# Decode attention with a parallel MLP on one core: the output weights laid 32 rows to a partition, the attention output computed whole at the end

## The chip, the core and the metric

The kernel runs on one core of a Trainium2 chip. The metric is the time of one execution in microseconds on the device, as the median of several runs. The core has a matrix engine (TensorE, "PE" in the profile, with its weight loads as "PEld"), a vector engine (VectorE, "DVE"), a scalar engine (ScalarE, "ACT"), a general engine (GpSimd, "POOL") and a queue engine (SyncE, "SP") that here issues nearly all transfers. 16 DMA engines carry the data from HBM into the on-chip memory SBUF (128 partitions). TensorE writes its results into PSUM, which has eight banks of 512 fp32 values per partition.

## What is computed

A decode step for 4 sequences with one token each, D = 576. The normalised input xn goes through grouped-query attention (32 query heads, 16 KV heads, head size 128) over the last 2048 cached positions, and through an MLP block with a gated-shift mixer; both are added to x.

```python
def _A_ref(x, k_cache, v_cache, wq, wo):
    W = min(4096, max(256, Sk // 4))                 # 2048
    q = (x @ wq).reshape(B, Sq, Hq, Dh).transpose(0, 2, 1, 3)
    k = jnp.repeat(k_cache[:, :, Sk - W:, :], rep, axis=1)
    v = jnp.repeat(v_cache[:, :, Sk - W:, :], rep, axis=1)
    p = _softmax(jnp.einsum("bhqd,bhkd->bhqk", q, k) * (Dh ** -0.5), axis=-1)
    o = jnp.einsum("bhqk,bhkd->bhqd", p, v)
    return o.transpose(0, 2, 1, 3).reshape(B, Sq, Hq * Dh) @ wo
...
xn = _layernorm(x, axis=-1)
return x + _A_ref(xn, A_k_cache, A_v_cache, A_wq, A_wo) + _B_ref(xn, B_w1, B_w2, B_w3, B_w4)
```

`_B_ref` makes x1 = xn + (shifted gelu(layernorm(xn) @ w1)) @ w2 and returns x1 + gelu(layernorm(x1) @ w3) @ w4. With one token the shifts leave only zeros. All tensors are bf16. The K and V windows are 33.6 MB each, wo and w4 are 4096 x 576 and 4608 x 576.

## The kernel before

Every step is registered with `add(engine, function, waits, sig, key)` or `add_dma`; for each engine the steps are sorted by their key, and each waits for the named steps by semaphores. So each engine's order is fixed by hand through the keys. Two loops of four turns each run on TensorE, one over K and one over V.

Nearly all transfers are issued by SP in one order (lines 213 to 252): wq, w1, w2, w3, then the 16 K tiles (one KV head for all four sequences, 2 MB, in runs of 16 KB: 128 partitions with 64 positions of 128 values each), V0 after K8, V1 to V3 after K15, then wo, V4 to V15, and w4 in four pieces (`W4P`: 14, 14, 6 and 2 rows of each partition's 36). K tiles go into a ring of four slots, V tiles into another; a tile's transfer waits until the slot's last reader is done. wo goes into the K ring once the second last K tile is transposed (`wo_wait`), w4 into the V ring after the matching PV step.

The K stage transposes the K tiles on TensorE (line 332), VectorE and ScalarE copy them out (340, 339), and TensorE makes the scores (348), four sequences at four column positions of the array. Then the softmax (374 to 400): maximum, exponentials, transposes; the reciprocal sums are spread over all partitions by a product with ones (405) and copied as `rinvB` (407). In the V stage step PV g (416) makes head pair g's outputs: 64 products with the V tile as weights, 8 columns (4 sequences x 2 heads). VectorE scales each result by `rinvB` into `OTn` (424) and prepares the next masked probabilities `PTg` (393).

The attention output product contracts 4096 rows (32 heads x 128) with wo. Here wo lies as `wo_sb[p, h, r, n]`, row h\*512 + p\*4 + r: eight blocks, each with four neighbouring rows per partition, in runs of 4.6 KB (line 239). The head outputs have to be brought into that order: `pe_sel` (434) picks every fourth value of a head dimension with a strided identity as weights, at four column positions, and VectorE copies the result as `ORT` (458). `pe_AO` (441, through the helper `acc_mm`) then makes for each block and r two products, one for each half of the 576 columns, into two accumulators `ACC` at column positions 0 and 32, in different banks. This is done in two parts (`AO_CH`): blocks 0 to 5 after PV11, inside the third turn's V loop by an `If` (48 products), blocks 6 and 7 after PV15 (16 products).

The same two accumulators take t1 = x + x1 through an identity (line 465) and the last MLP product with w4 (532; 28, 28, 12 and 4 products by piece). At the end VectorE and ScalarE copy one accumulator each (539, 540), and SP and ACT write them out.

```python
AO_CH = ((0, 6), (6, 8))
W4P = ((0, 14), (14, 28), (28, 34), (34, 36))
...
ACC = [ps[32 * k:32 * k + B, k, 0:HALF] for k in range(2)]
...
ins = e.matmul(ORps[32 * hh:32 * hh + 32, r, a:z, :], lhsT=ident_bf[:, r:128:4],
               rhs=ov[:, a:z, hh // 2, :, hh % 2], start=True, stop=True, ...)
...
ins = acc_mm(e, h, ORT[:, r, hg, :], wo_sb[:, hg, r, HALF * h:HALF * (h + 1)])
```

Of the kernel before, what the change touches and what calls it, by code (L numbers as in the profile page):

```python
# [5 lines left out]
FP32 = mybir.dt.float32  # L6
BF16 = mybir.dt.bfloat16
ACTF = mybir.ActivationFunctionType
ALU = mybir.AluOpType
AX = mybir.AxisListType  # L10
# [7 lines left out]
NIT = 4  # L18
ACT_EVAC = (1, 4, 7)
WO_AFTER = 3  # L20
V0_AFTER = 8
AO_CH = ((0, 6), (6, 8))
W4P = ((0, 14), (14, 28), (28, 34), (34, 36))


# [13 lines left out]
def bass_parallel_sum__sliding_block_cached__mixer_s_mlp__decode_kernel(  # L39
# [22 lines left out]
    with ExitStack() as ctx:  # L62
        def sb(name, shape, dt):
            return ctx.enter_context(nc.sbuf_tensor(name, shape, dt))
# [13 lines left out]
        w3rag = regB_t[:, 4 * F:W3E]  # L78
        wqmain = vring_t[:, 0:4 * Hq * Dh].rearrange("p (r n) -> p r n", r=4)
        wqrag = vring_t[:, 4 * Hq * Dh:4 * Hq * Dh + Hq * Dh // 2]  # L80
        wo_sb = kring_t[:, 0:Hq * D].rearrange("p (h r n) -> p h r n", h=8, r=4)
        _o = 4 * Hq * Dh + Hq * Dh // 2
        w1main = vring_t[:, _o:_o + 4 * D].rearrange("p (r n) -> p r n", r=4)
        _o += 4 * D
# [37 lines left out]
        rs4 = sb("rs4", [128, 4], FP32)  # L122
        rsum = sb("rsum", [128, 1], FP32)
        rinv = sb("rinv", [128, 1], FP32)
        rinvB = sb("rinvB", [128, 128], FP32)
        P_sb = sb("P_sb", [128, NT * 32], BF16)
        PTb = sb("PTb", [128, NT * 32], BF16)
        PTs = sb("PTs", [128, NT, 32], BF16)
        PTg = sb("PTg", [128, NPG, NT, B, 2], BF16)
        OTn = sb("OTn", [128, 128], BF16)  # L130
        ORT = sb("ORT", [128, 4, 8, B], BF16)
        t1 = sb("t1", [B, D], FP32)
        out_t = sb("out_sb", [32 + B, HALF], BF16)
        out_sb = [out_t[32 * h:32 * h + B, :] for h in range(2)]

        ps = ctx.enter_context(nc.psum_tensor("ps", [128, 8, 512], FP32))[:]
        Sps = ps[:, 0:4, :]
        tb = [ps[:, 4 + k, :].bitcast(BF16).rearrange("p (t d) -> p t d", t=8) for k in range(NTB)]
        ACC = [ps[32 * k:32 * k + B, k, 0:HALF] for k in range(2)]
        ORps = ps[:, 2, 0:128].rearrange("p (r h b) -> p r h b", r=4, h=8)  # L140
        rinvps = ps[:, 3, 0:128]
        OTps = lambda g: ps[:, 4 + g % 4, 0:8]
        Qps = ps[:, 0:2, :]
        Q_sb = P_sb[:, 0:1024]
# [18 lines left out]
        def add(engine, emit, waits=(), sig=None, key=0.0, loop=None):  # L163
            seqc[0] += 1
            prog[engine].append(Op(emit, waits, sig, key, seqc[0], loop))

        def add_dma(pairs, skey, waits=(), key=0.0, engine="sp"):
            if skey not in S:
                S[skey] = sem("s_" + "_".join(str(k) for k in (skey if isinstance(skey, tuple) else (skey,))))
            dma_count[skey] = dma_count.get(skey, 0) + 16 * len(pairs)  # L170

            def emit(e):
                for o_, i_ in pairs:
                    e.dma_start(o_, i_).then_inc(S[skey], 16)  # L174
            add(engine, emit, waits, None, key)
            return ("dma", skey, dma_count[skey])
# [57 lines left out]
        for g in range(G):  # L234
            kk = KS + g if g else V0_AFTER + 0.5
            w = [f"PV{g - NVS}"] if g >= NVS else (["hs1"] if g < WQ_SLOTS else [])
            ev_v.append(add_dma(kv_pairs(vring_t, g % NVS, A_v_cache, g), ("v", g % NVS), w, kk))
            if g == WO_AFTER:
                ev_wo = add_dma([(wo_sb.rearrange("p h r n -> p h (r n)"), A_wo.rearrange("(h p r) n -> p h (r n)", h=8, r=4))],
                                "wo", [wo_wait], kk + 0.1)  # L240
        w4_src = B_w4.rearrange("(p r) n -> p r n", r=RT)
        w4_sb = vring_t[:, 0:RT * D].rearrange("p (t n) -> p t n", n=D)
# [149 lines left out]
        for g in range(G):  # L392
# [11 lines left out]
        add("dve", lambda e: e.tensor_copy(out=bmask[:, :, 1], in_=bmask[:, :, 0]), waits=["bmask0"], sig="bmask", key=-40.9)  # L404
        add("pe", lambda e: e.matmul(rinvps, lhsT=ones_f[:], rhs=diag[:], start=True, stop=True), waits=["diag", "ones_f", "PTs3"],  # L405
            sig="rinvp", key=KS + 0.6)
        add("dve", lambda e: e.tensor_copy(out=rinvB[:].rearrange("p (g b e) -> p g b e", b=B, e=2),
                                           in_=rinvps.rearrange("p (b g e) -> p g b e", b=B, e=2)),
            waits=["rinvp"], sig="rinvB", key=KS + 0.6)


        def pe_PV(g):
# [7 lines left out]
        for g in range(G):  # L420
            m = g % 4
            add("pe", pe_PV(g), waits=[("L", ("v", m), 16), ("L", ("pg", m), 1), ("L", ("on", m), 1)], sig=f"PV{g}", key=KV + g,
                loop=("v", g // 4))
            add("dve", lambda e, g=g: e.tensor_tensor(out=OTn[:, 8 * g:8 * g + 8], in0=OTps(g), in1=rinvB[:, 8 * g:8 * g + 8], op=ALU.mult),  # L424
                waits=["rinvB", f"PV{g}"], sig=("on", m), key=KV + g + 0.5)


        def pe_sel(a, z):
            def f(e):
                ov = OTn[:].rearrange("p (h q b e) -> p h q b e", h=8, q=2, b=B)  # L430
                ins = None
                for r in range(4):
                    for hh in range(4):
                        ins = e.matmul(ORps[32 * hh:32 * hh + 32, r, a:z, :], lhsT=ident_bf[:, r:128:4],
                                       rhs=ov[:, a:z, hh // 2, :, hh % 2], start=True, stop=True,
                                       tile_position=(0, 32 * hh), skip_group_check=True)
                return ins
            return f

        def acc_mm(e, h, lhsT, rhs, start=False, stop=False):  # L440
            return e.matmul(ACC[h], lhsT=lhsT, rhs=rhs, start=start, stop=stop, tile_position=(0, 32 * h))  # L441

        def pe_AO(a, z):
            def f(e):
                ins = None
                for hg in range(a, z):
                    for r in range(4):
                        for h in range(2):
                            ins = acc_mm(e, h, ORT[:, r, hg, :], wo_sb[:, hg, r, HALF * h:HALF * (h + 1)])
                return ins  # L450
            return f
        for n, (a, z) in enumerate(AO_CH):
            last = z == 8
            kk = KV + (20 if last else 2 * z - 0.4)
            lp = None if last else ("v", NIT - 2, "only")
            add("pe", pe_sel(a, z), waits=[("c", ("on", (2 * z - 1) % 4), (2 * z - 1) // 4 + 2)] + ([f"ORT{n - 1}"] if n else []),
                sig=f"sel{n}", key=kk, loop=lp)
            add("dve", lambda e, a=a, z=z: e.tensor_copy(out=ORT[:, :, a:z, :], in_=ORps[:, :, a:z, :]),  # L458
                waits=[f"sel{n}"], sig=f"ORT{n}", key=kk)
            add("pe", pe_AO(a, z), waits=[f"ORT{n}"] + ([ev_wo] if n == 0 else []), sig=f"AO{n}", key=kk + 0.1, loop=lp)  # L460

        def pe_t1(e):
            ins = None
# [59 lines left out]
        add("act", gelu2, waits=["h2_4"], sig="gelu2", key=KW + 0.1)  # L523
        add("dve", lambda e: e.transpose(h2T_sb[:].rearrange("p c i -> p (c i)"), PTb[:, 0:N2]), waits=["gelu2"], sig="h2T", key=KW + 0.2)  # L524

        last_p = len(W4P) - 1
        for n, (t0, t1_) in enumerate(W4P):
            def f(e, t0=t0, t1_=t1_, hs=(0, 1)):
                ins = None
                for t in range(t0, t1_):  # L530
                    for h in hs:
                        ins = acc_mm(e, h, h2T_sb[:, t, 0:B], w4_sb[:, t, HALF * h:HALF * (h + 1)], stop=(t == RT - 1))
                return ins
            if n < last_p:
                add("pe", f, waits=[ev_w4[n], "h2T"], sig=f"MO{n}", key=KT + 20 + n)
            else:
                for h in range(2):
                    add("pe", lambda e, f=f, h=h: f(e, hs=(h,)), waits=[ev_w4[n], "h2T"], sig=f"MOl{h}", key=KT + 20 + n + 0.1 * h)
# [36 lines left out]
        def emit_program(eng_name, engine):  # L575
            waited = {}
            ops = prog[eng_name]
            k = 0
            while k < len(ops):
                op = ops[k]  # L580
                if op.loop is None:
                    emit_op(eng_name, engine, op, waited)
                    k += 1
                    continue
                name = op.loop[0]
                z = k
                while z < len(ops) and ops[z].loop is not None and ops[z].loop[0] == name:
                    z += 1
                group, k = ops[k:z], z
                shapes = [[o for o in group if o.loop[1] == it and len(o.loop) == 2] for it in range(NIT)]  # L590
                assert all([o.waits for o in sh] == [o.waits for o in shapes[0]] for sh in shapes)
                only = [o for o in group if len(o.loop) == 3]
                assert group[-2 * len(shapes[0]) - len(only):][len(shapes[0]):][:len(only)] == only
                with engine.Fori(0, NIT) as it:
                    for o in shapes[0]:
                        emit_op(eng_name, engine, o, waited, it)
                    if only:
                        with engine.If(it == only[0].loop[1]):
                            for o in only:
                                emit_op(eng_name, engine, o, waited, it)  # L600

        for name, eng in (("sp", nc.sync), ("pool", nc.gpsimd), ("dve", nc.vector), ("act", nc.scalar), ("pe", nc.tensor)):
            emit_program(name, eng)
# [28 lines left out]
```

## Time and profile before

| | |
|---|---|
| median of 3 runs | 217.0 us (217.07, 215.74, 217.0) |
| the profiled execution | 215.64 us, span 214.4 us |
| HBM read | 88.49 MB, 413 GB/s over the span |
| TensorE busy | 143.2 us (67%), mean granted clock 0.785 |
| VectorE, ScalarE, GpSimd busy | 84.5, 59.1, 10.0 us |
| share of the chain of waits by engine | DMA 53%, PE 36%, DVE 4%, SP 4% |

The span runs from the first to the last instruction. The chain of waits starts at the last instruction and goes back, at each step, to what released it; its entries are start, duration and what ran. A window row lists busy time and number of instructions for each engine, then the granted TensorE clock as a share of full speed, the mean busy share of the 16 DMA engines, and the rate of the transfers. A timeline row is start, duration, engine, line, operation, what it writes and reads, shapes and count; in brackets stands how long the engine had been idle before it, and what ended that.

### The profile page before, as it was taken

The page shows a single profiled execution, that of the slowest core. Times are in us where ns is not written, and L with a number is a line of the kernel's source. Part 1 is how long each engine was busy: PE and PEld are TensorE (multiplying, and loading weights), DVE is VectorE, ACT ScalarE, POOL GpSimd, SP SyncE. Part 2 cuts the span into 40 slices and gives each one's busy share as a digit, 9 for nine tenths or more (in the row PEclk, how much of TensorE's full clock was granted, in tenths as well). Part 3 has the DMA queues.
Part 4 walks back from the last instruction along what each step waited for, and adds up shares of the span by engine and source line. Part 5 has one row for each costly group of instructions (what it writes and reads, how often), then busy time and mean ns, then how long its engine had stood idle before and what let it go on. Part 6 is the DMA issues. An engine that isn't in the chain of part 4 may idle for free.

```text
span 214.4 us, 5735 instructions
## 1 busy us (share of the span) xinstructions
PE 143.2 (67%) x2646; PEld 109.1 (51%) x2648; DVE 84.5 (39%) x162; ACT 59.1 (28%) x71; POOL 10.0 (5%) x34
## 2 busy tenths in 40 slices
PE   0368375999999993999999719813343443973655
PEld 0115223777788883788877604813343443463523
DVE  5502603666666663466666479411111112100000
ACT  2000302566555553365666653000000000000000
POOL 8101000000010000000000000000000000000000
PEclk9999755999999999699999985555555555585589
DMA  6999999999999999999999999999999999999992
GB/s 245 434 395 439 440 410 437 428 408 431 428 431 422 431 428 434 422 434 423 431 425 431 428 407 411 424 427 431 419 434 431 431 419 434 428 434 421 424 412 113
DMA packets 7697, 88.63 MB, mean 413 GB/s; under 512 B 764, under 2 KB 1032, under 8 KB 2824
## 3 DMA queue, kind: packets, MB, share of 16 engines
q1 hardware_dynamic: 7672, 88.50, 97.8%
q8 instruction: 7, 0.11, 0.2%
q14 instruction: 2, 0.02, 0.0%
q10 hardware_dynamic: 16, 0.01, 0.0%
HBM read 88.49 MB, written 0.00 MB: 413 GB/s over the span
## 4 chain that ended last, share of the span: by engine, by line
DMA 53%; PE 36%; DVE 4%; SPq 4%; issue 2%; ACT 0%
DMA vring<-in_A_v_cache_dram 25%; PE ps L332 23%; DMA kring<-in_A_k_cache_dram 21%; PE ps L348 7%; DMA vring<-in_B_w_dram 7%; PE ps L416 5%; SPq L174 4%; DVE PTb L382 1%; DVE rmax L374 1%; DVE regB L340 1%; PE ps L441 1%; DVE PTs L390 1%; PE ps L405 0%; ACT P_sb L379 0%; DVE out_sb L539 0%
## 5 line engine op out<-in xcount | busy, mean ns | idle before, releaser
L340 DVE COPY regB<-ps 128x1024 bf16<-128x1024 bf16 x80 | 52.3, 687 | 34.7 <-PE ps L332 32.9
L332 PEld LDWEIGHTS ps<-perm_k,kring 128*128 128x128 bf16 x1024 | 58.7, 99 | 12.6 <-issue 8.7
L332 PE MATMUL ps<-perm_k,kring 128*128 128x128 bf16 x1024 | 62.1, 222 | 4.2 <-DMA kring<-in_A_k_cache_dram 4.2
L339 ACT ACTIVATE regB<-ps 128x1024 bf16<-128x1024 bf16 x48 | 47.7, 1023 | 41.4 <-PE ps L332 41.4
L416 PE MATMUL ps<-PTg,vring 128*128 128x8 bf16 x1024 | 29.2, 168 | 33.3 <-DMA vring<-in_A_v_cache_dram 31.4
L416 PEld LDWEIGHTS ps<-PTg,vring 128*128 128x128 bf16 x1024 | 28.1, 103 | 34.5 <-DMA vring<-in_A_v_cache_dram 24.3
L424 DVE TENSOR_TENSOR OTn<-ps,rinvB 128x8 bf16<-128x8 f32 x16 | 2.7, 167 | 57.3 <-PE ps L416 57.2
L540 ACT ACTIVATE out_sb<-ps 4x288 bf16<-4x288 f32 x1 | 0.4, 402 | 81.2 <-PE ps L441 81.2
L348 PE MATMUL ps<-regB,Qs 128*32 128x512 bf16 x272 | 18.7, 395 | 4.6 <-issue 3.5
L348 PEld LDWEIGHTS ps<-regB,Qs 128*32 128x32 bf16 x272 | 6.6, 97 | 10.8 <-issue 6.2
L393 DVE TENSOR_TENSOR PTg<-PTs,bmask 128x512 bf16<-128x512 bf16 x16 | 10.7, 682 | 0.0
L370 POOL COPY Qs<-Qpad 128x128 bf16<-128x128 bf16 x16 | 4.6, 296 | 93.5 <-PE ps L348 81.4
L441 PE MATMUL ps<-kring,ORT 128*4 128x288 bf16 x64 | 7.7, 431 | 0.7 <-DVE ORT L458 0.7
L441 PE MATMUL ps<-vring,h2T_sb 128*4 128x288 bf16 x72 | 5.3, 299 | 2.8 <-DMA vring<-in_B_w_dram 2.8
L511 PE MATMUL ps<-regB,x1nT 128*32 128x432 bf16 (+1 forms) x60 | 5.4, 522 | 2.1 <-DMA regB<-in_B_w_dram 1.6
L274 PE MATMUL ps<-ident_bf,xn_bf 4*128 4x4 bf16 x8 | 0.5, 169 | 8.8 <-DVE ragsrc L267 8.8
L296 PE MATMUL ps<-vring,xnT 128*32 128x512 bf16 x40 | 4.6, 629 | 1.8 <-DMA vring<-in_A_wq_dram 1.8
L441 PEld LDWEIGHTS ps<-kring,ORT 128*4 128x4 bf16 x64 | 3.8, 121 | 3.9 <-DVE ORT L458 0.9
L441 PEld LDWEIGHTS ps<-vring,h2T_sb 128*4 128x4 bf16 x72 | 3.0, 87 | 5.3 <-DMA vring<-in_B_w_dram 4.0
L383 PE MATMUL ps<-PTb,perm_p 128*128 128x512 bf16 x3 | 1.8, 608 | 4.9 <-DVE PTb L382 4.8
L274 PEld LDWEIGHTS ps<-ident_bf,xn_bf 4*128 4x128 bf16 x8 | 0.4, 112 | 8.8 <-POOL ones_f L210 6.3
L524 DVE STREAM_TRANSPOSE h2T_sb<-PTb 128x1152 bf16<-128x1152 bf16 x1 | 1.4, 1378 | 8.4 <-ACT PTb L521 8.4
(88 smaller groups left out, 61.7 us busy)
## 6 DMA issues: line engine op xcount, KB each, us to landing
kring<-in_A_k_cache_dram SPq DMA_DIRECT2D x16, 2048.0 KB, 16.1
vring<-in_A_v_cache_dram SPq DMA_DIRECT2D x16, 2048.0 KB, 17.6
regB<-in_B_w_dram SPq DMA_DIRECT2D x2, 2304.0 KB, 21.3
kring<-in_A_wo_dram SPq DMA_DIRECT2D x1, 4608.0 KB, 24.1
vring<-in_A_wq_dram SPq DMA_DIRECT2D x2, 2048.0 KB, 9.5
vring<-in_B_w_dram SPq DMA_DIRECT2D x2, 2016.0 KB, 15.7
vring<-in_B_w_dram SPq DMA_DIRECT2D x2, 576.0 KB, 13.8
vring<-in_B_w_dram SPq DMA_DIRECT2D x1, 864.0 KB, 14.7
```

Source lines behind the costliest of these rows:

```text
L174: e.dma_start(o_, i_).then_inc(S[skey], 16)
L296: ins = e.matmul(Qps[32 * j:32 * j + 32, k, :], lhsT=x_, rhs=w, start=(r == 0), stop=(r == 4), tile_position=(0, 32 * j))
L332: ins = e.transpose(tb[n % NTB][:, t, :], kring[:, g % NKS, 8 * k + t, :], perm_k[:])
L339: return "act", lambda e: e.activation(out=ktbuf[:, n % NKT], in_=src, func=ACTF.Copy)
L340: return "dve", lambda e: e.tensor_copy(out=ktbuf[:, n % NKT], in_=src)
L348: ins = e.matmul(Sps[32 * b:32 * b + 32, c4, :].rearrange("p (t i) -> p t i", t=16), lhsT=Qs[:, g % 4, b, :], rhs=kttile[:, t0:t0 + 16, b, :],
L370: P(lambda e, g=g: e.tensor_copy(out=Qs[:, g % 4], in_=Qpad[:, g]), waits=(["qT"] if g == 0 else []) + ([f"SC{g - 4}"] if g >= 3 else []), ...
L393: add("dve", lambda e, g=g: e.tensor_tensor(out=PTg[:, g % NPG], in0=PTs[:, :, 2 * g:2 * g + 2].unsqueeze(2).to_broadcast([128, NT, B, 2]) ...
L416: ins = e.matmul(OTps(g), lhsT=vring[:, g % NVS, t, :], rhs=PTg[:, g % NPG, t].rearrange("p b e -> p (b e)"), start=(t == 0), stop=(t == N ...
L424: add("dve", lambda e, g=g: e.tensor_tensor(out=OTn[:, 8 * g:8 * g + 8], in0=OTps(g), in1=rinvB[:, 8 * g:8 * g + 8], op=ALU.mult), waits=[ ...
L441: return e.matmul(ACC[h], lhsT=lhsT, rhs=rhs, start=start, stop=stop, tile_position=(0, 32 * h))
L511: ins = e.matmul(H2ps[k][32 * j:32 * j + 32, :], lhsT=x_, rhs=w, start=(r == 0), stop=(r == 4), tile_position=(0, 32 * j))
```

## The change

wo is laid out with 32 neighbouring rows on each partition, so that each partition receives one run of 36,864 bytes. Partition p then holds a quarter of one head: head p // 4, values 32 (p % 4) to 32 (p % 4) + 31.

The head outputs are brought into this order in another way. A mask `qmask[d, q]` is 1 where d // 32 = q. The reciprocal sums are multiplied by it, `rinvM`, so that the scaling of each PV result writes each value four times, three of them as zeros (`OTx`). `pe_turn` then makes four products, one for each sequence, with `OTx` as weights (128 columns: 32 heads x 4 quarters) and `sel32`, four identities of 32 one under the other; the result has (head, quarter) on the partitions and the 32 values of the quarter along the row. One copy makes `ORT` of it.

The attention output is made whole after PV15: 64 products into four accumulators, two for each half (even and odd r), at four column positions. The first w4 piece (t < FOLD = 14) uses the same four. Then ScalarE copies the two added accumulators to SBUF, and two fp32 products with an identity add them to the first two; the rest is as before. `rinvM` and `OTx` use the memory of `PTb`, `fold_sb` that of `P_sb`. The mask is made by VectorE near the start, `sel32` by three additions on GpSimd.

```diff
-AO_CH = ((0, 6), (6, 8))
+FOLD = 14
...
-        wo_sb = kring_t[:, 0:Hq * D].rearrange("p (h r n) -> p h r n", h=8, r=4)
+        wo_sb = kring_t[:, 0:32 * D].rearrange("p (r n) -> p r n", r=32)
...
-        ACC = [ps[32 * k:32 * k + B, k, 0:HALF] for k in range(2)]
+        ACC = [ps[32 * k:32 * k + B, min(k, 2), 0:HALF] for k in range(4)]
...
-                ev_wo = add_dma([(wo_sb.rearrange("p h r n -> p h (r n)"), A_wo.rearrange("(h p r) n -> p h (r n)", h=8, r=4))],
+                ev_wo = add_dma([(kring_t[:, 0:32 * D], A_wo.rearrange("(p r) n -> p (r n)", r=32))],
                                 "wo", [wo_wait], kk + 0.1)
...
-        add("dve", lambda e: e.tensor_copy(out=rinvB[:]..., in_=rinvps...), waits=["rinvp"], sig="rinvB", key=KS + 0.6)
+        add("dve", lambda e: e.tensor_tensor(
+            out=rinvM.rearrange("p b h q -> p (b h) q"),
+            in0=rinvps.unsqueeze(2).to_broadcast([128, 128, 4]),
+            in1=qmask[:].unsqueeze(1).to_broadcast([128, 128, 4]), op=ALU.mult),
+            waits=["rinvp", "qmask"], sig="rinvM", key=KS + 0.6)
+        add("dve", lambda e: e.tensor_reduce(out=qmask[:], in_=ident_bf[:].rearrange("p (q r) -> p q r", q=4), axis=AX.X, op=ALU.add),
+            waits=["ident_bf"], sig="qmask", key=-40.8)
+        add("pool", lambda e: e.tensor_tensor(out=sel32[:], in0=ident_bf[:, 0:32], in1=ident_bf[:, 32:64], op=ALU.add),
+            waits=["ident_bf"], sig="sel_a", key=-88)
...
+            add("dve", lambda e, g=g: e.tensor_tensor(
+                out=OTx[:, :, 2 * g:2 * g + 2, :], in0=OTps(g).rearrange("p (b e) -> p b e", b=B).unsqueeze(3).to_broadcast([128, B, 2, 4]),
+                in1=rinvM[:, :, 2 * g:2 * g + 2, :], op=ALU.mult),
+                waits=["rinvM", f"PV{g}"], sig=("on", m), key=KV + g + 0.5)
+        def acc_mm(e, h, lhsT, rhs, start=False, stop=False, k0=0):
+            return e.matmul(ACC[h], lhsT=lhsT, rhs=rhs, start=start, stop=stop, tile_position=(k0, 32 * h))
+        def pe_AO(e):
+            ins = None
+            for r in range(32):
+                for h in range(2):
+                    ins = acc_mm(e, 2 * (r % 2) + h, ORT[:, r:128:32], wo_sb[:, r, HALF * h:HALF * (h + 1)], start=(r == 1))
+            return ins
+        def pe_turn(e):
+            ins = None
+            for b in range(B):
+                ins = e.matmul(ORps[:, 32 * b:32 * b + 32], lhsT=OTx[:, b].rearrange("p h q -> p (h q)"), rhs=sel32[:], start=True, stop=True)
+            return ins
+        add("pe", pe_turn, waits=[("c", ("on", m), NIT + 1) for m in range(4)] + ["sel32"], sig="turn", key=KV + 19.9)
+        add("dve", lambda e: e.tensor_copy(out=ORT[:], in_=ORps), waits=["turn"], sig="ORT", key=KV + 20)
+        add("pe", pe_AO, waits=["ORT", ev_wo], sig="AO", key=KV + 20)
...
+        def pe_fold(e):
+            ins = None
+            for h in range(2):
+                k0 = 64 + 32 * h
+                ins = acc_mm(e, h, ident_f[k0:k0 + B, k0:k0 + B], fold_sb[k0:k0 + B, :], k0=k0)
+            return ins
+        add("act", lambda e: e.activation(out=fold_sb[64:96 + B, :], in_=ps[64:96 + B, 2, 0:HALF], func=ACTF.Copy),
+            waits=[f"MO{n_fold}"], sig="foldc", key=KT + 20 + n_fold + 0.5)
+        add("pe", pe_fold, waits=["foldc"], sig="fold", key=KT + 20 + n_fold + 0.5)
...
-                        ins = acc_mm(e, h, h2T_sb[:, t, 0:B], w4_sb[:, t, HALF * h:HALF * (h + 1)], stop=(t == RT - 1))
+                        a = 2 * (t % 2) + h if t < FOLD else h
+                        ins = acc_mm(e, a, h2T_sb[:, t, 0:B], w4_sb[:, t, HALF * h:HALF * (h + 1)], stop=(t == RT - 1 or (t == FOLD - 1 and a > 1)))
```

More of the change, by code (lines that the diff above doesn't have):

```diff
@@ L124, in bass_parallel_sum__sliding_block_cached__mixer_s_mlp__decode_kernel @@
         rinv = sb("rinv", [128, 1], FP32)
-        rinvB = sb("rinvB", [128, 128], FP32)
         P_sb = sb("P_sb", [128, NT * 32], BF16)
@@ L129, in bass_parallel_sum__sliding_block_cached__mixer_s_mlp__decode_kernel @@
         PTg = sb("PTg", [128, NPG, NT, B, 2], BF16)
-        OTn = sb("OTn", [128, 128], BF16)
-        ORT = sb("ORT", [128, 4, 8, B], BF16)
+        rinvM = PTb[:, 0:1024].bitcast(FP32).rearrange("p (b h q) -> p b h q", b=B, q=4)
+        OTx = PTb[:, 1024:1536].rearrange("p (b h q) -> p b h q", b=B, q=4)
+        qmask = sb("qmask", [128, 4], FP32)
+        sel32 = sb("sel32", [128, 32], BF16)
+        ORT = sb("ORT", [128, 128], BF16)
         t1 = sb("t1", [B, D], FP32)
+        fold_sb = P_sb[:, 0:2 * HALF].bitcast(FP32)
         out_t = sb("out_sb", [32 + B, HALF], BF16)
@@ L138, in bass_parallel_sum__sliding_block_cached__mixer_s_mlp__decode_kernel @@
         tb = [ps[:, 4 + k, :].bitcast(BF16).rearrange("p (t d) -> p t d", t=8) for k in range(NTB)]
-        ACC = [ps[32 * k:32 * k + B, k, 0:HALF] for k in range(2)]
-        ORps = ps[:, 2, 0:128].rearrange("p (r h b) -> p r h b", r=4, h=8)
+        ACC = [ps[32 * k:32 * k + B, min(k, 2), 0:HALF] for k in range(4)]
         rinvps = ps[:, 3, 0:128]
+        ORps = ps[:, 3, 128:256]
         OTps = lambda g: ps[:, 4 + g % 4, 0:8]
@@ L406, in bass_parallel_sum__sliding_block_cached__mixer_s_mlp__decode_kernel @@
             sig="rinvp", key=KS + 0.6)
-        add("dve", lambda e: e.tensor_copy(out=rinvB[:].rearrange("p (g b e) -> p g b e", b=B, e=2),
-                                           in_=rinvps.rearrange("p (b g e) -> p g b e", b=B, e=2)),
-            waits=["rinvp"], sig="rinvB", key=KS + 0.6)
+        add("dve", lambda e: e.tensor_tensor(
[7 more added lines that the diff above has]
+            waits=["ident_bf"], sig="sel_a", key=-88)
+        add("pool", lambda e: e.tensor_tensor(out=sel32[:], in0=sel32[:], in1=ident_bf[:, 64:96], op=ALU.add),
+            waits=["sel_a"], sig="sel_b", key=-87.9)
+        add("pool", lambda e: e.tensor_tensor(out=sel32[:], in0=sel32[:], in1=ident_bf[:, 96:128], op=ALU.add),
+            waits=["sel_b"], sig="sel32", key=-87.8)
         def pe_PV(g):
@@ L423, in bass_parallel_sum__sliding_block_cached__mixer_s_mlp__decode_kernel @@
                 loop=("v", g // 4))
[L424 to L460, printed above, removed]
+            add("dve", lambda e, g=g: e.tensor_tensor(
+                out=OTx[:, :, 2 * g:2 * g + 2, :], in0=OTps(g).rearrange("p (b e) -> p b e", b=B).unsqueeze(3).to_broadcast([128, B, 2, 4]),
+                in1=rinvM[:, :, 2 * g:2 * g + 2, :], op=ALU.mult),
+                waits=["rinvM", f"PV{g}"], sig=("on", m), key=KV + g + 0.5)
@@ L524, in bass_parallel_sum__sliding_block_cached__mixer_s_mlp__decode_kernel @@
         add("dve", lambda e: e.transpose(h2T_sb[:].rearrange("p c i -> p (c i)"), PTb[:, 0:N2]), waits=["gelu2"], sig="h2T", key=KW + 0.2)
+        def pe_fold(e):
[4 more added lines that the diff above has]
+            return ins
+        n_fold = [z for _, z in W4P].index(FOLD)
+        assert FOLD % 2 == 0
+        add("act", lambda e: e.activation(out=fold_sb[64:96 + B, :], in_=ps[64:96 + B, 2, 0:HALF], func=ACTF.Copy),
+            waits=[f"MO{n_fold}"], sig="foldc", key=KT + 20 + n_fold + 0.5)
+        add("pe", pe_fold, waits=["foldc"], sig="fold", key=KT + 20 + n_fold + 0.5)
         last_p = len(W4P) - 1
@@ L589, in emit_program @@
                 group, k = ops[k:z], z
-                shapes = [[o for o in group if o.loop[1] == it and len(o.loop) == 2] for it in range(NIT)]
+                shapes = [[o for o in group if o.loop[1] == it] for it in range(NIT)]
                 assert all([o.waits for o in sh] == [o.waits for o in shapes[0]] for sh in shapes)
-                only = [o for o in group if len(o.loop) == 3]
-                assert group[-2 * len(shapes[0]) - len(only):][len(shapes[0]):][:len(only)] == only
                 with engine.Fori(0, NIT) as it:
@@ L596, in emit_program @@
                         emit_op(eng_name, engine, o, waited, it)
[L597 to L600, printed above, removed]
         for name, eng in (("sp", nc.sync), ("pool", nc.gpsimd), ("dve", nc.vector), ("act", nc.scalar), ("pe", nc.tensor)):
```

## The prediction

> **What bounds the kernel now.** I read the page's slices first, then the chain of waits, then windows of DMA rate, then the timeline of the tail.
>
> ```profile
> span 214.4 us, 5735 instructions
> ...
> PEclk9999755999999999699999985555555555585589
> DMA  6999999999999999999999999999999999999992
> ```
>
> The DMA row is at 9 in 38 of 40 slices: the transfers never stop between the first and the last slice, whatever the engines do.
>
> ```profile
> 176.96 17.62 DMA vring<-in_A_v_cache_dram
> ...
> 194.62 1.88 PE ps L416 x64
> ...
> 196.53 14.69 DMA vring<-in_B_w_dram
> ...
> 211.26 1.20 PE ps L441 x16
> 212.46 0.43 DVE out_sb L539
> ```
>
> The chain of waits ends in transfers: the last w4 piece lands at 211.22 (196.53 + 14.69), and behind it lie only 16 products and a copy. So a change counts if it shortens the stream of transfers, or if it makes TensorE miss the last landing.
>
> ```profile
> core 0: us, PE busy (x) PEld busy (x) DVE busy (x) ACT busy (x) POOL busy (x), PEclk, DMA share, GB/s
> 17.00:27.00 10.00, 6.71 (x53) 3.77 (x54) 3.98 (x15) 1.86 (x4) 0.77 (x3) 0.86 0.99 421
> 18.00:24.00 6.00, 3.76 (x20) 1.97 (x17) 2.49 (x10) 0.20 (x1) 0.77 (x3) 1.00 1.03 439
> 36.00:122.00 86.00, 78.44 (x1280) 64.94 (x1280) 52.21 (x80) 46.96 (x48) 3.85 (x13) 0.97 1.01 428
> 127.00:138.00 11.00, 9.15 (x220) 6.65 (x222) 8.85 (x20) 3.40 (x10) 0.00 (x0) 0.50 1.01 407
> 143.00:193.00 50.00, 24.16 (x704) 20.75 (x704) 6.61 (x19) 0.00 (x0) 0.00 (x0) 0.53 1.01 428
> ```
>
> The last column is the rate. K and V travel in runs of 16 KB (64 rows of 128 bf16) at 428 GB/s, in both long windows. The one long stretch that is lower, 407, is where wo passes.
>
> ```profile
> 116.69 0.39 SPq L174 DMA_DIRECT2D kring<-in_A_wo_dram  x1
> 134.27 48.11 SPq L174 DMA_DIRECT2D vring<-in_A_v_cache_dram  x12
> ...
> kring<-in_A_wo_dram SPq DMA_DIRECT2D x1, 4608.0 KB, 24.1
> ```
>
> wo is issued at 116.69 and lands 24.1 us later, at 140.8; it lies behind V1 to V3 in the one queue, so its own bytes pass in the last 11 to 12 us of that, where the rate is low. Its runs are 4 rows of 576 bf16, 4.6 KB.
>
> **The transfer of wo.** 4608 KB are 4.72 MB: at 407 GB/s 11.59 us. Runs of 37 KB do not occur before, so their rate is bounded. At the 428 of 16 KB runs it is 11.02 us, 0.57 less; w3, whose runs are 18 KB with the same 37 KB from one partition's rows to the next's, passes between 17 and 27 us by the 6 MB ahead of it in the queue, and gives 421 (0.38 less) over all of it and 439 (0.84 less) in its best part. I take 428, the long average and between w3's two: **-0.57 us**. A loss is unlikely because w3 has the same spacing in HBM and is not below 421. All later transfers stand behind wo in the queue, and none of them waits for it: V4 is issued at 134.27, when PV0 is done, 6.5 us before wo lands, and so it goes on with each V. So the saving reaches the end whole: the last w4 would land at 210.65 instead of 211.22.
>
> The Trainium skill, "DMA: Bandwidth & Descriptors", section "Why small descriptors are slow (HBM only)", gives about 3 cycles for each packet beside its 32-byte beats: 144 beats for 4608 bytes, 1152 for 36,864, so an estimate from that page of 1.8% of wo's time, or 0.2 us. The trace's gap of 5% between 407 and 428 is larger than this rule makes it.
>
> **The tail on TensorE.** This is where the change adds work.
>
> ```profile
> 182.84 5.62 PE L441 MATMUL ps<-kring,ORT 128*4 128x288 bf16 x48 [0.45 <-DVE ORT L458]
> ...
> 199.53 1.87 PE L416 MATMUL ps<-PTg,vring 128*128 128x8 bf16 x64 [3.03 <-DMA vring<-in_A_v_cache_dram]
> ...
> 201.43 0.17 DVE L424 TENSOR_TENSOR OTn<-ps,rinvB 128x8 bf16<-128x8 f32 x1 [4.73 <-PE ps L416]
> ...
> 201.65 0.30 PE L434 MATMUL ps<-OTn,ident_bf 128*32 128x8 bf16 x16 [0.26 <-DVE OTn L424]
> 202.01 0.19 DVE L458 CAST ORT<-ps 128x32 bf16<-128x32 f32 x1 [0.41 <-PE ps L434]
> ...
> 202.25 2.08 PE L441 MATMUL ps<-kring,ORT 128*4 128x288 bf16 x16 [0.30 <-DVE ORT L458]
> ...
> 204.34 2.23 PE L441 MATMUL ps<-vring,h2T_sb 128*4 128x288 bf16 x28
> ...
> 209.17 1.88 PE L441 MATMUL ps<-vring,h2T_sb 128*4 128x288 bf16 x28 [2.60 <-DMA vring<-in_B_w_dram]
> ...
> 211.26 1.15 PE L441 MATMUL ps<-vring,h2T_sb 128*4 128x288 bf16 x16 [0.20 <-DMA vring<-in_B_w_dram]
> ```
>
> Three quarters of the attention product (48 of 64) now run at 182.84, beside transfers; 16 run in the tail at 202.25, then the first w4 piece's 28, then TensorE waits 2.60 for the second piece. After the change nothing runs at 182.84 and all 64 come after V15. Two rates are read here, with two accumulators in turn: 5.62/48 = 117 ns a product at the half clock, 1.88/28 = 67 ns at the full one. Removing the 48 gains nothing itself: w4's first issue waits for PV12, which these 48 hold up, and can come sooner, but V15 ahead of it in the queue lands only at 199.5 (PV15's wait for it).
>
> With four accumulators at four column positions I expect four products at once:
>
> ```profile
> 28.63 2.11 PE L511 MATMUL ps<-regB,x1nT 128*32 128x432 bf16 x24 [1.12 <-DMA regB<-in_B_w_dram]
> ...
> 122.81 1.05 PE L348 MATMUL ps<-regB,Qs 128*32 128x512 bf16 x16 [1.16 <-DVE regB L340]
> 130.58 1.12 PE L441 MATMUL ps<-t,ident_f 4*4 4x288 f32 x4
> ```
>
> L511 and L348 write four column positions in turn. L511 passes 16 times 432 and 8 times 288 columns, 9216, in 2.11 us at the half clock, 0.229 ns a column; L348 8192 in 1.05 us at the full one, 0.128. For 288 columns that is 66 and 37 ns.
>
> Now the tail, on the time scale of before. PV15 ends at 201.40. The scaling by rinvM writes 32 values instead of 8: about 0.2 (0.17 above). Four products of 32 columns: at most the 0.30 of the 16 at L434. The copy of 128x128 is as large as that at L407 below, 0.28. With the four hand-overs of 0.05 the first attention product starts near 202.4, 0.15 later than now. At the half clock until 205.1 there is room for 41 products, the other 23 at 37 ns take 0.85: end 205.95. The 28 of the first w4 piece, four ways, 1.04: 207.0. Then the fold: an ACT copy of 36x288 (the output's copies of 4x288 take about 0.4, the same length), and two fp32 products; t1's two take 1.12 at the half clock and so 0.56 at the full one. With hand-overs it ends at 208.1. The second w4 piece is there at 208.6 (209.17 - 0.57). So TensorE waits again, 0.5 us, and the end is again the transfers': the term is **0**, with a cover of 0.5, and 0.2 more behind the second piece.
>
> **The rest.**
>
> ```profile
> 1.87 0.28 DVE L402 TENSOR_REDUCE bmask<-ident_bf 128x4 f32<-128x128 bf16 x1 [1.87 <-POOL ident_bf L189]
> ...
> 13.04 2.75 PE L296 MATMUL ps<-vring,xnT 128*32 128x512 bf16 x24 [1.78 <-DMA vring<-in_A_wq_dram]
> ...
> 134.03 0.28 DVE L407 COPY rinvB<-ps 128x128 f32<-128x128 f32 x1
> ...
> 145.92 1.85 PE L416 MATMUL ps<-PTg,vring 128*128 128x8 bf16 x64 [4.57 <-DMA vring<-in_A_v_cache_dram]
> ```
>
> The quarter mask is one more reduction like L402, 0.28 us, ahead of the first layer norm; even if nothing nearer covers it, it ends in L296's wait of 1.78 for wq. The three POOL additions stand behind all that POOL prepares early, and their result is read only in the tail. The reciprocals at L407 grow from 128 to 512 values: by 0.28 a 128 at most 1.1 us, 0.8 more. Behind that on VectorE stand the scaling of PV0 and the mask of the fifth V; PV4 is only due at 145.92. Cost 0 for these.
>
> **The sum.** The profiled execution took 215.64 us, 1.24 beyond its span. 215.64 - 0.57 + 0 = 215.07. It is an execution of the lower kind: the runs were 217.07, 215.74 and 217.0. What the upper ones have more has to be settled to forecast a median.
>
> ```profile
> 188.00:188.50 0.50, 0.50 (x12) 0.20 (x7) 0.00 (x0) 0.00 (x0) 0.00 (x0) 0.98 0.77 328
> ...
> 191.00:191.50 0.50, 0.50 (x26) 0.50 (x23) 0.00 (x0) 0.00 (x0) 0.00 (x0) 0.94 0.92 393
> ...
> 205.00:205.20 0.20, 0.20 (x6) 0.15 (x4) 0.00 (x0) 0.00 (x0) 0.00 (x0) 0.78 1.13 484
> ```
>
> The granted clock (third from the right) is only ever 0.5 or 1, so these means place the changes: up at 188.02, down at 191.44, up at 205.09. The distances are 3.42 and 17.07, five times 3.41: the clock changes on a grid of 3.41 us. In the tail it went up at 205.09, after 2.8 us of products. Had the grid lain so that the tail's 44 products (5.1 us at 117 ns) filled no step well enough, the second w4 piece would have begun at the half clock: 28 products 3.3 instead of 1.88, up to 1.9 more with the last 16, about 1 where the clock comes up among them. That puts such runs at 216.6 to 217.5, and 217.0 lies there.
>
> The Trainium skill, "TensorE: Matmul & The Clock Gate", section "What's actually happening", says that this window is free-running and does not start with the kernel. The trace agrees on the window (3.41 us here, 3413 ns there); that its place differs from run to run one trace can't show.
>
> **Forecast and rivals.** One per cent of 217.0, 2.2 us, is about what can be told from no change.
>
> Forecast, 0.56: wo passes 0.57 sooner, and the tail's stream, now 96 products and denser, from 202.4 to 208.1, fills a step of the clock at any place of the grid, so that all runs end like the profiled one: **215.1**, 0.9% under 217.0. Its own range is 214.7 to 215.5, from the rates of w3 and a little scatter.
>
> Rival one, 0.22: the upper runs have another cause and keep their 1.3 us. Then the median is 217.0 - 0.57 = 216.4. For it: one profile says nothing of the other runs.
>
> Rival two, 0.16, slower: TensorE becomes the end. It decides once attention and first w4 piece together take over 5.1 us (208.6 less 202.4 and the fold's 1.1; 4.6 in my sum). If the four column positions run only two at a time: 64 products to 207.9 (23 at 117, 41 at 67), 28 to 209.7, fold 210.8, 28 to 212.7, 16 to 213.8, against 212.4 now: 217.1 (0.07). If four at once but at the half clock throughout: 64 at 66 ns to 206.6, 208.4, fold 210.0, then 28 and 16 at 117 to 215.2: 218.4 (0.05). Both: 223 (0.04). For it speaks that clock row 5 fills the V stage; against it L511 and L348, and the clock's rise at 205.09 from less work.
>
> Rival three, 0.06: the 407 isn't due to run length (V and softmax meet there too), and 37 KB runs pass no faster: 215.6 to 217.0.
>
> **Numbers.** Faster by over 1% is under 214.8: three in ten of the forecast, where wo gains near 0.84 or the median of before comes out at the upper kind's top, and a little of unknown gains: 0.2. Slower by over 1% is over 219.2: the worst part of rival two, the half-clock part where before's median falls to the lower kind, and a remainder for what I don't see: 0.11. The rest, 0.69, within. The range holds forecast, rivals one and three, and the first part of two: 214.4 to 217.3.
>
> **What would show it.** After, in the windows: the rate where wo passes at 421 to 439 instead of 407, its landing 0.4 to 0.8 sooner from issue. In the timeline: 64 products from about 202 in some 3.6 us, 28 in about 1.0, the fold, and then a wait for w4's second piece; the last 16 released by DMA, at 210.7. Runs that agree within 0.3 us would speak for the clock grid. Wrong it is if the wait ahead of the second piece is gone or released by the fold (rival two), if wo's stretch stays at 407, or if runs still lie 1.3 us apart.

## The result, and the profile after

| | before | changed kernel |
|---|---|---|
| median of 20 runs each | 215.82 us | 215.28 us |
| lowest to highest | 215.62 to 217.14 | 215.17 to 216.71 |
| runs above 216.4 | 8 of 20 | 2 of 20 |
| ratio | | 0.9961, 95% interval 0.9945 to 0.9976 |

The change makes the kernel faster by 0.4%. That is less than the 1% that the prediction called hard to tell from no change, and less than half of the 0.9% that it forecast. The forecast was 215.1, the range 214.4 to 217.3. The times fall into two groups, about 1.3 us apart, in both kernels; the median of the 3 runs known before (217.0) lay in the upper one, the median of 20 in the lower one. So the median falls by 0.25% only, while the ratio, which goes by the means and so also sees that fewer runs lie in the upper group, is 0.39% under 1.

Of the profile after, first the windows in which wo and most of V pass (columns as before: the last is the rate in GB/s):

```profile
127.00:138.00 11.00, 7.79 (x160) 5.01 (x160) 7.33 (x17) 1.90 (x5) 0.00 (x0) 0.50 1.01 433
143.00:193.00 50.00, 19.57 (x670) 18.71 (x669) 7.49 (x20) 0.00 (x0) 0.00 (x0) 0.50 1.00 427
```

The dip is gone: 433 where there was 407, and V as before (427, it was 428). The issue of wo, and its time from issue to landing:

```profile
115.19 0.33 SPq L177 DMA_DIRECT2D kring<-in_A_wo_dram  x1
...
kring<-in_A_wo_dram SPq DMA_DIRECT2D x1, 4608.0 KB, 25.1
```

wo lands at 140.3, half a microsecond sooner than before, though 25.1 us after its issue and not 24.1: in this run it was issued 1.5 us sooner. The timeline of TensorE's tail:

```profile
199.18 1.87 PE L429 MATMUL ps<-PTg,vring 128*128 128x8 bf16 x64 [3.02 <-DMA vring<-in_A_v_cache_dram]
...
201.53 0.27 PE L455 MATMUL ps<-sel,PTb 128*128 128x32 bf16 x4 [0.48 <-DVE PTb L437]
201.84 0.29 DVE L458 CAST ORT<-ps 128x128 bf16<-128x128 f32 x1 [0.56 <-PE ps L455]
...
202.18 4.01 PE L444 MATMUL ps<-kring,ORT 128*4 128x288 bf16 x64 [0.38 <-DVE ORT L458]
...
205.98 1.21 PE L444 MATMUL ps<-vring,h2T_sb 128*4 128x288 bf16 x28
207.25 0.41 ACT L533 ACTIVATE P_sb<-ps 36x288 f32<-36x288 f32 x1 [77.50 <-PE ps L444]
...
207.71 0.65 PE L444 MATMUL ps<-P_sb,ident_f 4*4 4x288 f32 x4 [0.52 <-ACT P_sb L533]
...
208.84 1.88 PE L444 MATMUL ps<-vring,h2T_sb 128*4 128x288 bf16 x28 [0.49 <-DMA vring<-in_B_w_dram]
...
210.92 1.15 PE L444 MATMUL ps<-vring,h2T_sb 128*4 128x288 bf16 x16 [0.20 <-DMA vring<-in_B_w_dram]
```

The 64 products take 4.01 us, 63 ns each, all at the half clock (it rose at 206.35), where two accumulators took 117 ns each. TensorE is through with the fold at 208.36 and waits 0.49 us for the second w4 piece. The last 16 are released by a transfer at 210.92 instead of 211.26. The end is still the transfers', as the chain of waits after says:

```profile
196.19 14.69 DMA vring<-in_B_w_dram
210.88 0.04 issue
210.92 1.20 PE ps L444 x16
212.12 0.43 DVE out_sb L550
```

### The profile page after: what moved, and what is told of

Its sections match the earlier page's. It is cut to its first block, busy times and chain, and to the rows that moved or that the text cites. A ratio compares the mean times of both kernels' runs of the same rounds, so it can differ in the third digit from the quotient of the medians.

```text
span 214.1 us, 5690 instructions
## 1 busy us (share of the span) xinstructions
PE 139.0 (65%) x2624; PEld 106.6 (50%) x2624; DVE 85.2 (40%) x162; ACT 59.8 (28%) x72; POOL 10.7 (5%) x37
## 4 chain that ended last, share of the span: by engine, by line
DMA 52%; PE 36%; DVE 4%; SPq 4%; issue 3%; ACT 0%
DMA vring<-in_A_v_cache_dram 24%; PE ps L335 23%; DMA kring<-in_A_k_cache_dram 21%; PE ps L351 7%; DMA vring<-in_B_w_dram 7%; PE ps L429 5%; SPq L177 4%; DVE PTb L385 1%; DVE rmax L377 1%; DVE regB L343 1%; PE ps L444 1%; DVE PTs L393 1%; PE ps L408 0%; ACT P_sb L382 0%; DVE out_sb L550 0%
## 5 line engine op out<-in xcount | busy, mean ns | idle before, releaser
L335 PEld LDWEIGHTS ps<-perm_k,kring 128*128 128x128 bf16 x1024 | 58.1, 98 | 13.1 <-issue 9.3
L437 DVE TENSOR_TENSOR PTb<-ps,PTb 128x32 bf16<-128x32 f32 x16 | 3.1, 192 | 57.8 <-PE ps L429 57.8
L386 PE MATMUL ps<-PTb,perm_p 128*128 128x512 bf16 x4 | 2.4, 607 | 4.3 <-DVE PTb L385 4.1
L444 PE MATMUL ps<-vring,h2T_sb 128*4 128x288 bf16 x72 | 4.2, 298 | 0.7 <-DMA vring<-in_B_w_dram 0.7
L444 PE MATMUL ps<-kring,ORT 128*4 128x288 bf16 x64 | 4.0, 443 | 0.4 <-DVE ORT L458 0.4
L263 ACT ACTIVATE sd<-mv 4x1 f32<-4x1 f32 x3 | 0.6, 202 | 12.4 <-DVE mv L261 12.4
## 6 DMA issues: line engine op xcount, KB each, us to landing
kring<-in_A_wo_dram SPq DMA_DIRECT2D x1, 4608.0 KB, 25.1
```

Source lines behind the costliest of these rows:

```text
L335: ins = e.transpose(tb[n % NTB][:, t, :], kring[:, g % NKS, 8 * k + t, :], perm_k[:])
L437: add("dve", lambda e, g=g: e.tensor_tensor(out=OTx[:, :, 2 * g:2 * g + 2, :], in0=OTps(g).rearrange("p (b e) -> p b e", b=B).unsqueeze(3) ...
```

## The experiments

Each was timed beside runs of the kernel before. In every kernel with two groups over 0.6 us lie empty between them. "Lower median" is the median of the runs of the lower group alone; for before it was 215.72 to 215.76 beside every set of experiments.

| kernel | runs | median | lower median | upper group |
|---|---|---|---|---|
| before, all sets | 124 | 215.80 | 215.73 | 48 |
| before, once more | 12 | 215.76 | 215.75 | 2 |
| changed kernel, two sets | 32 | 215.28, 215.31 | 215.28, 215.29 | 5 |
| before with 37 KB runs | 12 | 215.36 | 215.26 | 3 |
| change with 4.6 KB runs | 12 | 215.75 | 215.75 | 0 |
| before with 2.3 KB runs | 10 | 216.82 | 216.30 | 5 |
| change with two accumulators | 12 | 216.05 | one spread, 215.22 to 216.43 | |
| before without 28 products | 10 | 217.61 | none | 10 |
| before with 12 products more | 12 | 215.76 | 215.76 | 0 |
| change with 8 products more, two sets | 24 | 215.25, 215.28 | 215.25, 215.28 | 0 |

**The run length alone, put into before.**

```diff
-ev_wo = add_dma([(wo_sb.rearrange("p h r n -> p h (r n)"), A_wo.rearrange("(h p r) n -> p h (r n)", h=8, r=4))],
+ev_wo = add_dma([(kring_t[:, 0:Hq * D], A_wo.rearrange("(p r) n -> p (r n)", r=32))],
```

> The kernel before with one change: wo's transfer takes 37 KB runs into the same bytes of SBUF (the rows of wo then lie in another order than the products take them, so the attention output is another sum). Theory (run length): the stretch of wo passes at 427 to 433 GB/s instead of 407, all later landings come about 0.57 us sooner, and the time falls by 0.3 to 0.6 us against before, as much as or more than the whole change gave (0.5). Two groups of times 1.3 us apart stay, since the tail on TensorE is untouched. Rival (the gain came from the tail or from freeing the V loop of 48 products): within 0.15 us of before.

Measured: lower median 215.26, 0.47 under before's; the upper group stays (216.21 to 216.57, 3 of 12). The window of wo, in its profile:

```profile
127.00:138.00 11.00, 7.71 (x160) 5.04 (x161) 6.90 (x17) 1.87 (x5) 0.00 (x0) 0.50 1.02 436
```

With the tail and the V loop of before, the run length gives as much to the lower group as the whole change.

**The run length alone, taken out of the change.**

```diff
-ev_wo = add_dma([(kring_t[:, 0:32 * D], A_wo.rearrange("(p r) n -> p (r n)", r=32))],
+ev_wo = add_dma([(kring_t[:, 0:32 * D].rearrange("p (h x) -> p h x", h=8), A_wo.rearrange("(h p r) n -> p h (r n)", h=8, r=4))],
```

> The changed kernel with wo's transfer back in 4.6 KB runs into the same bytes (rows in another order, so another sum). Theory (run length): the stretch of wo is back at 407, the lower group of times is back at that of before, 215.6 to 216.0; the upper group stays as rare as with the change (2 of 20), because the tail is that of the change. Rival (tail or loop): the time stays at 215.2 to 215.4.

Measured: 215.63 to 215.93, all 12 in the lower group, which is back at that of before; wo's window:

```profile
127.00:138.00 11.00, 8.51 (x190) 5.85 (x191) 7.67 (x17) 1.86 (x4) 0.00 (x0) 0.50 1.01 409
```

So the change has two effects that can be had apart: the run length moves the lower group, and with the new tail the upper one is rarer. With these 12, 5 of 44 runs with the new tail lie in it, against 48 of 124 of before.

**Twice as many runs.** In before, the same line with `h=16, r=2`.

> The kernel before with wo in runs of 2.3 KB (two rows), 2048 of them instead of 1024 (rows in another order, so another sum). Theory (each run costs a fixed time beside its bytes; from 0.57 us for 896 runs fewer, or 56 fewer on each of 16 engines, 10 ns a run): 64 more runs on each engine cost 0.6 us, the lower group lies at 216.2 to 216.5, and wo's stretch passes at some 385 GB/s. The Trainium skill, DMA: Bandwidth & Descriptors, section Why small descriptors are slow (HBM only), gives 3 cycles a packet; by that estimate 0.2 to 0.3 us. Rival (4.6 KB runs are a special case): within 0.15 us of before.

```profile
127.00:138.00 11.00, 10.05 (x232) 6.94 (x233) 9.08 (x20) 3.11 (x8) 0.00 (x0) 0.50 1.04 387
```

Lower median 216.30, 0.57 above before's, at 387 GB/s. If the runs are spread evenly over the 16 engines, these are 64 more on each, at 8.9 ns a run; for the 56 fewer of the change, 0.47 us is 8.4. The two agree, in both directions from 4.6 KB, so the cost goes with the number of runs and 4.6 KB is no special case. (With the bytes fixed, more runs are also shorter ones; the two can't be told apart here.)

The first tile behind wo is V4, and where TensorE waits for it its product starts when it lands; here with 37 KB (the changed kernel), then with 2.3 KB:

```profile
145.44 1.85 PE L429 MATMUL ps<-PTg,vring 128*128 128x8 bf16 x64 [0.86 <-DMA vring<-in_A_v_cache_dram]
```

```profile
146.49 1.85 PE L416 MATMUL ps<-PTg,vring 128*128 128x8 bf16 x64 [5.45 <-DMA vring<-in_A_v_cache_dram]
```

In all profiles in which TensorE waited for V4 that product starts at 145.33 to 145.48 with 37 KB (four profiles), at 145.91 to 146.06 with 4.6 KB (five) and at 146.49 with 2.3 KB (one). So all of the difference is there once wo has passed, whatever the tail is.

**Two accumulators instead of four, no fold.**

```diff
-ins = acc_mm(e, 2 * (r % 2) + h, ORT[:, r:128:32], wo_sb[:, r, HALF * h:HALF * (h + 1)], start=(r == 1))
+ins = acc_mm(e, h, ORT[:, r:128:32], wo_sb[:, r, HALF * h:HALF * (h + 1)])
...
-a = 2 * (t % 2) + h if t < FOLD else h
+a = h
```

> The changed kernel with two accumulators throughout: the 64 attention products and the first w4 piece's 28 go to two column positions, and the fold is gone. Theory (four column positions hide the tail): attention and first piece take 7.3 us instead of 4.8 and end near 209.5, past the second piece's landing at 208.8, so the second piece begins late by 0.7 and the last 16 products begin at about 211.4 to 211.6 released by TensorE: 0.5 to 0.8 us slower than the change, with a wider scatter as the clock's rise falls early or late. Rival (the tail is hidden anyway): as fast as the change, within 0.15 us.

Measured: median 216.05, 0.77 over the change; the runs are spread from 215.22 to 216.43, where four of the 12 lie. Its profiled run (216.20), first in the timeline, then in the chain of waits:

```profile
202.06 6.48 PE L444 MATMUL ps<-kring,ORT 128*4 128x288 bf16 x64 [0.38 <-DVE ORT L458]
208.37 4.57 PE L444 MATMUL ps<-vring,h2T_sb 128*4 128x288 bf16 x72
```

```profile
202.01 0.04 issue
202.06 10.94 PE ps L444 x112
213.00 0.43 DVE out_sb L547
```

No wait for w4 is left: one stream of TensorE from 202.06 to the end. This is what the prediction's rival two feared, that TensorE becomes the end, and it shows that in most runs the four column positions are what keeps the whole attention output out of the path. The fastest of the 12 is no slower than the change.

**Before, once more, for a run of the upper group.**

> The kernel before, unchanged, for the span and mean granted clock of each single run. Theory (clock grid in the tail): the runs near 217.0 differ from those near 215.8 in the tail: the second w4 piece or the last 16 products run at the half clock. If the profile falls on such a run it shows 28 products in over 2.5 us from about 209.2, or 16 in over 1.7. Rival (another cause): the tail's rows are the same in both, and the 1.3 us are lost earlier, in the landings of the K or V tiles.

10 of 12 runs lay in the lower group, 2 in the upper, and the profile fell on a lower one, so the question stayed open here. Yet its rows show the clock's rise at another place than before's profile: the first w4 piece took 3.37 us instead of 2.23, and in the windows below the clock rose only at 207.5 (it was 205.09).

```profile
204.45 3.37 PE L441 MATMUL ps<-vring,h2T_sb 128*4 128x288 bf16 x28
209.29 1.88 PE L441 MATMUL ps<-vring,h2T_sb 128*4 128x288 bf16 x28 [1.47 <-DMA vring<-in_B_w_dram]
```

```profile
207.00:207.50 0.50, 0.50 (x8) 0.27 (x4) 0.00 (x0) 0.00 (x0) 0.00 (x0) 0.50 0.92 387
207.50:208.00 0.50, 0.32 (x4) 0.00 (x0) 0.00 (x0) 0.00 (x0) 0.00 (x0) 0.98 0.95 401
```

This costs nothing, since the clock is up when the second piece begins.

**Less work in before's tail.** The first w4 piece's 28 products are left out.

> The kernel before without the first w4 piece's 28 products (they are left out, all transfers stay). TensorE does less in the tail. Theory (clock grid): with only 2.4 us of products between PV15 and the second piece no step of 3.41 us is filled, the clock stays at a half, the second piece's 28 products take 3.3 us instead of 1.88, and nearly all runs lie in the upper group, 216.7 to 217.7, or up to 1.9 above the lower group of before. Rival (the upper group comes from elsewhere): the two groups stay in the shares of before, about 60 and 40 in 100, or the time falls.

```profile
202.35 2.08 PE L441 MATMUL ps<-kring,ORT 128*4 128x288 bf16 x16 [0.30 <-DVE ORT L458]
209.27 5.01 PE L441 MATMUL ps<-vring,h2T_sb 128*4 128x288 bf16 x44 [4.83 <-DMA vring<-in_B_w_dram]
```

All 10 runs lie between 216.74 and 218.01, median 217.61: 28 products fewer, and 1.9 us slower than before's lower group. The last 44 products begin with the transfer as ever, but take 5.01 us; in the windows the granted clock is 0.5 up to 213.5.

**More work in before's tail.** After the first w4 piece:

```diff
+def pe_fill(e):
+    for _ in range(6):
+        for h in range(2):
+            ins = e.matmul(ps[32 * h:32 * h + B, 3, 0:HALF], lhsT=h2T_sb[:, 0, 0:B], rhs=w4_sb[:, 0, HALF * h:HALF * (h + 1)],
+                           start=True, stop=True, tile_position=(0, 32 * h))
+    return ins
+add("pe", pe_fill, waits=["rinvB"], sig="fill", key=KT + 20.5)
```

> The kernel before with 12 more products of 4x288 between the first and the second w4 piece, into a part of PSUM that nobody reads, so that TensorE has more to do in the tail, 0.8 to 1.4 us, all of it before the second piece lands. Theory (clock grid): the stretch of products grows from 5.1 to 6.5 us at the half clock, and fills a step at nearly any place of the grid; the upper group shrinks from about 4 in 10 runs to 1 in 10 or none, the lower group stays at 215.6 to 216.0. Rival: the shares stay, or all runs are slower.

Measured: all 12 runs between 215.69 and 215.85. With before's share of 48 in 124 in the upper group, none in 12 would come by chance in 3 of 1000 cases. Useless products remove the upper group, and missing ones make every run at least as slow: before's upper group is the tail at the half clock. No run of that group was profiled, so this rests on the two experiments and not on its rows.

**The change again, and the change with 8 more products.** The same function with `range(4)`, between the first w4 piece and the fold.

> The changed kernel with 8 more products of 4x288, into a part of PSUM that nobody reads, in the 0.52 us in which TensorE waits for ScalarE's copy before the fold. Theory (clock grid): the one gap in the tail's stream closes, no run is left in an upper group, and the lower group stays at 215.2 to 215.45: as fast as the change and without its 1 run in 10 near 216.6. Rival: the 8 products push the fold past the second piece's landing and all runs are up to 0.3 slower.

> The changed kernel itself, unchanged, beside the one above: 215.2 to 215.45, and about 1 run in 10 at 216.5 to 216.7. If the profile falls on one of those: the clock's rise comes only after the fold, so that the fold is late and the second piece's products run at the half clock for a part (theory), or the tail is as in the other runs and the landings are later (rival).

The unchanged copy had 3 of 12 runs at 216.46 to 216.57, and its profile fell on one of these. TensorE's tail in the timeline, then two stretches of windows (granted clock third from the right):

```profile
205.66 1.03 PE L444 MATMUL ps<-vring,h2T_sb 128*4 128x288 bf16 x28
207.20 0.65 PE L444 MATMUL ps<-P_sb,ident_f 4*4 4x288 f32 x4 [0.51 <-ACT P_sb L533]
208.70 4.53 PE L444 MATMUL ps<-vring,h2T_sb 128*4 128x288 bf16 x44 [0.85 <-DMA vring<-in_B_w_dram]
```

```profile
205.00:205.50 0.50, 0.50 (x16) 0.30 (x12) 0.00 (x0) 0.00 (x0) 0.00 (x0) 0.57 1.14 484
...
208.50:209.00 0.50, 0.30 (x4) 0.20 (x6) 0.00 (x0) 0.00 (x0) 0.00 (x0) 0.84 1.09 420
209.00:209.50 0.50, 0.50 (x7) 0.27 (x4) 0.00 (x0) 0.00 (x0) 0.00 (x0) 0.50 0.71 286
```

The fold was not late, against my expectation. The clock rose at 205.43, early, and fell at 208.84, one step of 3.41 later, 0.14 us after the second piece had begun: in that step TensorE had finished the big products by 206.69 and run only the short fold. The last 44 products took 4.53 us at the half clock. So this run of the upper group is one whose clock rises early and falls again. The change with 4.6 KB runs has the same tail, and in its profile (215.74, lower group) the clock rose at 205.57 and stayed up: 1.46 us of the big products lay in that step, here 1.26. With the 8 products in the gap none of 12 runs lay in the upper group (215.12 to 215.66), so 12 more were run:

> The same kernel as in the run with the 8 more products, once more, because 12 runs without a value near 216.6 would come out by chance in 13 of 100 cases if 5 in 32 had stayed. Theory (clock grid): again none above 216, the median at 215.2 to 215.35. Rival: one or more of 12 at 216.4 to 216.7.

215.21 to 215.53, so none in 24. If 5 in 32 were the exact rate of the change, that would come by chance in 17 of 1000 cases. But 5 in 32 is a sample too: with that, 24 runs without one come by chance in 5 of 100 cases, and in 10 of 100 if the 12 runs with 4.6 KB, which have the same tail and none in the upper group, are counted with it. So it is likely and not shown that the 8 products empty the upper group. They cost nothing: the lower group is that of the change.

## Why the prediction was right, point by point

- **wo's transfer.** The mechanism was right, the size too large: 0.57 was taken from 407 against 428 GB/s, the lower groups give 0.45 (215.73 to 215.28), the run length alone 0.47 in either direction. That is halfway between the average of 16 KB runs that I took and the lower of w3's two rows (0.38). That the size came so near is in part luck. The rate rose further than I took, to 433 and 436, which by the same sum would be 0.7 or more; and w3's rows, my bounds, are 428 and 433 in the changed kernel's profile, where the same transfer had given 421 and 439. A window's rate gives the saving only to some 0.2 us. One sign was wrong: wo's landing was to come 0.4 to 0.8 sooner from its issue, and came 1.0 later, because that time also depends on when wo is issued. The rule of The Trainium skill, "DMA: Bandwidth & Descriptors", "Why small descriptors are slow (HBM only)", gave an estimate of 0.2, which is less than half of what was measured.
- **The tail on TensorE.** The sum gave 207.0 for the end of the first piece, 208.1 for the fold, 0.5 of waiting; measured 207.19, 208.36 and 0.49. That they agree so well is luck, since two errors cancel. The sum moved the second piece's landing 0.57 sooner and left the tail's start where it was, though V15 stands behind wo too. And it had the clock's rise where before's profile had it; in the run after it came at 206.35 (the mean of the half microsecond from 206.0 is 0.65), and the attention product took 4.01 us instead of 3.6. In the profiles of the same tail with an earlier rise TensorE waits 0.85 us (205.43) and 1.05 (205.57).
- **The edits at nothing.** The multiplication by the mask took 0.68 us (bound 1.1), the scaling of a PV result 0.19 (0.2). Making the mask took 2.24 us instead of 0.28; it was still covered, since the first product with wq begins at 9.36 in both profiles. Run length alone gives the whole gain, so none of them costs anything that shows.
- **The two groups.** That the upper one is the clock grid in the tail is shown by taking products away and adding some. Wrong was "all runs end like the profiled one": 5 of 32 do not, and "runs still lie 1.3 us apart" was one of the prediction's own signs of being wrong. The forecast counted whether the stream fills a step, and not that the clock falls after a step that is not filled; the fold opens that gap itself.
- **The level.** Three runs, two of them upper, made me take before's level as 217.0 and the change as 0.9% of it. By 124 runs 4 in 10 are upper, and the ratio is 0.9961. The time came out right because the lower group was worked out by itself, from the profiled execution.
- **The rivals.** One (the upper runs have another cause) falls by the two experiments on before's tail and by the profiled upper run of the change; two (TensorE becomes the end) appears when the accumulators are taken away; three (37 KB runs pass no faster) falls.

What stays open: how much activity raises the clock and keeps it up. In before's profile 1.5 us of products in a step held it, and so did 1.46 us and the fold in the change with 4.6 KB; in the copy of the change 1.26 us and the fold did not. Nor does being busy alone raise it: in before TensorE ran the PV products, 8 columns each, without a pause from 133 to 138 at a granted clock of 0.50.

## What to carry to other kernels

Where the transfers never stop, a transfer's number of runs is a price like its bytes: here some 9 ns a run on each of 16 engines, whoever waits for that data. Work moved into a tail under transfers was free here only because its products ran at four column positions, so the cover should be worked out for the rate they reach, and at the half clock too. And where a few products end the kernel, what TensorE did in the microseconds before decides how fast they are: 12 products that nobody reads took away 1.2 us from 4 runs in 10 of before, at no cost to the others. A median of three runs can lie in either group.

## What I had not expected

A clock that rises early in the tail can be worse than one that rises late. In before's copy it was up at 207.5, and the run was of the lower group; in the change's copy it was up at 205.43 and down again by the time it was needed. (It is not early or late alone: in before's own profile it rose at 205.09, and more products in that step held it.)
